# Another planned order for attention and two feed-forward stages, and x blocks at other addresses

## The chip, the cores and the metric

The kernel runs on one core of one Trainium2 chip. The metric is device time in microseconds (us) of one execution; of several executions the median counts.

## The reference

Three stages follow one another. First, block-causal attention over 4 batches, 8 heads, 576 positions and 64 values a head. Then a feed-forward with softmax-weighted linear units and a layer norm on 2304 tokens (512 to 1024 to 512), and a second feed-forward with Mish (512 to 2048 to 512).

```python
scores = scale * np.matmul(q, k.transpose(0, 1, 3, 2))     # masked by blocks of 64 positions
attn = softmax(scores); x = np.matmul(attn, v)             # to (2304, 512)
...
h = x @ w_in; solu = h * softmax(h)
ln = (solu - mean) / sqrt(var + 1e-06) * g_ln; x = ln @ w_out
...
h = x @ w2_in; g = h * tanh(softplus(h)); out = g @ w2_out
```

Inputs are float32, the weights float64.

## The kernel before

**Arithmetic.** Every large matmul is made of three in a shorter float format: an operand is split into a high part and the remainder (`h` and `l`), and high x high, low x high and high x low are summed in PSUM. The weights arrive as pairs of 32-bit words and are put together on the chip by a chain of some ten operations on DVE (VectorE), ACT (ScalarE) and POOL (GpSimd): L423 and L425 take the exponent and the mantissa apart, L467 and L477 to L482 put them together, L319, L325 and L328 split them.

**Stages.** Attention goes over 16 pairs of heads (`pair`, index p): loads of K, Q and V by SP, turns of K and Q on PE (TensorE) at L640, scores at L665, maxima on DVE, exponentials on ACT (L677), scaling on POOL (L733), turns of the result (L749) and the product with V (L770, L777). The first feed-forward takes 18 tiles of 128 tokens (`moe1_tile`: L833, L880) and 9 groups of two (`moe1_x2`: L896). Its result goes to DRAM. The second feed-forward (`moe2_group`, `moe2_pair`) goes in two halves over the hidden dimension; each half has five token groups (512, 512, 256, 512 and 512 tokens) and four pairs of hidden tiles. It computes the first product by a scheme of seven block products in place of eight (`prod`, L1055: six matmuls of 256 columns each), with ACT copies (L1063) and DVE adds (L1067) between them, then Mish, a split on ACT and DVE, and the output matmuls of 512 columns (L1112). Where a group has 256 tokens there are four products.

**The x blocks.** `moe2_x` reads x from DRAM (L1127), takes differences on DVE (L1132), and splits seven blocks into high parts (ACT, L319) and low parts (POOL, L328). They go to ten rotating buffers of each kind, `blk_h` and `blk_l`: 0 to 5 in the pool opened on the right after attention, 6 and 7 in the room of the first feed-forward's weights `wih` and `wil`, 8 and 9 in the pool opened on the left. Each buffer of the two pools is 528 values long, of which 512 are used, so that neighbours differ by 64 bytes modulo 512. The weights of the second feed-forward all start at 192 modulo 512. Blocks 0 to 5 start at 192, 256, 320, 384, 448 and 0 (both kinds), blocks 6 and 7 at 64 and 128, the high parts 8 and 9 at 192 and 256, and the low parts 8 and 9 at 320 and 384.

**The order.** Nothing in the program's order is written by hand. `add` collects operations (3 to 24 instructions of one engine for PE, mostly one for the others) with an engine, a cost in us, the keys read and written, a priority `prio`, and the PSUM banks they take and give back. `Plan.order` replays them in planned time: each engine takes, of the operations that are ready, the one with the lowest priority number. The result is a static order: on the chip each engine's instructions run in that order, and an instruction that waits holds all that stand behind it on its engine. An operation counts as ready when its inputs have ended and a latency of the producing engine has passed (`LAT`: PE, DVE, ACT, POOL, SP, host). The costs are formulas in the number n of values a partition (`c_dve`, `c_act`, `c_ts` and `c_tt` for POOL, `c_dma`). Operations of DVE with `lock`, most of those with operands in SBUF alone, and all of POOL hold one common lock, so that planned time never has one of DVE beside one of POOL.

**Priorities.** `PRIO` gives each tag a base and a step; the priority is base + step x index, the index being the pair of heads, the tile, the weight chunk (0 to 31) or the pair of tiles of the second feed-forward (0 to 39). Tags with `_b` belong to the pairs from 8 on. The tags of which the text speaks: `load_k`, `load_q`, `load_v` (SP), `wir`, `wor`, `w2ar`, `w2br` (reads of weights, SP), `wi`, `wo`, `w2a`, `w2b` (their conversion; `w2a` is for the first two sets of the second feed-forward), `f_x`, `f_t`, `f_s` (x: reads, differences, splits), `f_h` (products), `f_c` (copies), `f_d` (adds), `f_v`, `f_p`, `f_q` (Mish and the split of the hidden values), `f_o` (output matmuls).

The step that the adds take in `moe2_pair`:

```python
add(DVE, c_dve(256), lambda: nc.vector.tensor_tensor(
    out=part(x, i), in0=ps(s)[:, 0:256], in1=part(x, i), op=ALU.add),
    r=[key], w=[x.key(i)], rel=rel, prio=pri("f_d", cnt))
```

Of the kernel before, what the change touches and what calls it, by code (L numbers as in the profile page):

```python
# [26 lines left out]
PRIO = {  # L27
    "load_k": (3584270706, 49.53508582), "load_q": (3584552413, 2.997211538), "load_v": (3584552852, 30.17666404),
# [6 lines left out]
    "w2b": (3584800363, 0.1223531397), "m_x": (3584270481, -7.359126932), "m_h": (3584466166, -2.254093813),  # L35
    "m_v": (3584270377, 9.357429256), "m_w": (3584557870, 6.33404786), "m_u": (3584465474, 5.654352939),
    "m_s": (3584597059, 68.68855867), "m_l": (3584472153, 4.127067276), "m_t": (3584270485, -1.604672924),
    "m_e": (3584598271, 13.20145894), "m_2": (3584466906, 1.251409589), "m_o": (3584597866, 3.694405243),
    "store": (3584271882, 2.346070517), "load_k_b": (3584466375, -0.4078997786),
    "load_q_b": (3584466378, 0.8395418885), "load_v_b": (3584559519, -2.172838748), "tr_b": (3584270603, 85.63069486),  # L40
    "te_b": (3584466669, 21.88305874), "sc_b": (3584464169, 134.7168412), "mx_b": (3584598175, 8.054664166),
    "ex_b": (3584270568, 1.479017813), "su_b": (3584598230, 0.00851345384), "nm_b": (3584552091, 66.60840871),
    "pt_b": (3584270636, -0.9432254557), "pe_b": (3584270488, 0.2673815775), "pv_b": (3584464031, 70.47618497),
    "po_b": (3584269612, 69.4503458), "f_x": (3584558387, 3.529061523), "f_t": (3584466403, -0.8489929687),
    "f_s": (3584552262, 55.84067482), "f_h": (3584559956, 25.46036702), "f_c": (3584270484, -0.9543860343),
    "f_d": (3584269368, 3.538408075), "f_v": (3584464336, 40.97717236), "f_p": (3584465168, 9.220698474),
    "f_q": (3584466866, 0.03331880098), "f_o": (3584589259, 357.8175481), "f_a": (3584465747, 4.127067276),
    "f_e": (3584271879, 2.346070517),
}
# [17 lines left out]
class Plan:  # L67

    LAT = (0.21, 0.07, 0.07, 0.1, 2.4, 0.0)

# [196 lines left out]
def c_tt(n):  # L269
    return (110 + 2.3 * n) / 960.0  # L270


@with_exitstack
def kernel(
# [26 lines left out]
    NBLK = 10  # L301
    EDGE = 104
    NRIGHT = 6
# [91 lines left out]
    def weight(raws, ems, src, tag, idx, paths, after=(), pair=False):  # L395
# [21 lines left out]
        def dst():  # L417
# [4 lines left out]
            r=after, w=[rk], prio=pri(tag + "r", idx))  # L422
        add(DVE, (78 + wd / 2) / 960, lambda: nc.vector.tensor_scalar(ex(), hi(), 0x7FF00000, None, op0=ALU.bitwise_and),  # L423
            r=[rk], w=[ek], prio=pri(tag, idx), lock=True)
        add(DVE, (78 + wd / 2) / 960, lambda: nc.vector.tensor_scalar(  # L425
            ma(), hi(), 0xFFFFF, 0x100000, op0=ALU.bitwise_and, op1=ALU.bitwise_or), r=[rk], w=[mk], prio=pri(tag, idx), lock=True)
# [150 lines left out]
    def pair(p, xt):  # L577
        b, h2 = divmod(p, HP)

        def pri(tag, i):  # L580
            base, step = PRIO[tag if p < 8 else tag + "_b"]
            return base + step * i
# [85 lines left out]
        def sums(ts):  # L668
            a, n_ = ts
            c = [sm.key(x, t) for x in range(2) for t in range(a, a + n_)]  # L670
            add(DVE, 0.12, lambda: nc.vector.tensor_scalar(
                sm.t[:, :, a:a + n_], sm.t[:, :, a:a + n_], 1e-9, None, op0=ALU.add), w=c, prio=pri("su", p))
            add(DVE, 0.1, lambda: nc.vector.reciprocal(sm.t[:, :, a:a + n_], sm.t[:, :, a:a + n_]), w=c, prio=pri("su", p))  # L673
# [130 lines left out]
    def moe1_tile(i, xts, lth, ltl):  # L804
# [40 lines left out]
        def both(t):  # L845
# [6 lines left out]
            r=[hk, st.key(0)], w=[st.key(2), e.key()], prio=pri("m_w", i))  # L852
        add(DVE, 0.12, lambda: nc.vector.tensor_scalar(c(2), c(2), 1e-9, None, op0=ALU.add), w=[st.key(2)], prio=pri("m_u", i))
        add(DVE, 0.12, lambda: nc.vector.reciprocal(c(2), c(2)), w=[st.key(2)], prio=pri("m_u", i))
# [3 lines left out]
        add(DVE, 0.12, lambda: nc.vector.tensor_scalar(c(4), c(4), -1.0 / DFF, None, op0=ALU.mult),  # L858
            w=[st.key(4)], prio=pri("m_u", i))
# [3 lines left out]
        add(DVE, 0.12, lambda: nc.vector.tensor_scalar(c(6), c(6), 1.0 / DFF, 1e-6, op0=ALU.mult, op1=ALU.add),  # L863
            w=[st.key(6)], prio=pri("m_s", i))
# [86 lines left out]
    def open_right():  # L951
# [11 lines left out]
        for r in (blk_h, blk_l):  # L963
# [12 lines left out]
    def open_left():  # L976
# [4 lines left out]
        for j in range(3, NSLOT):  # L981
            slot(p, j)
        for r in (gh_r, gl_r, blk_h, blk_l, ob_r):
            r.make(p)
        for r in (blk_h, blk_l):
            r.tiles = [t[:, 0:512] for t in r.tiles]

# [47 lines left out]
    def moe2_pair(cnt, half, g, m, first, last, xs, oslots):  # L1035
# [12 lines left out]
        def prod(k, a, b, s, key, start):  # L1048
            xb, xl = xs[b]

            def go():
# [226 lines left out]
```

## Time and profile before

| what | value |
|---|---|
| median of 3 runs | 809.52 us (806.14, 811.68, 809.52) |
| profiled execution | 808.99 us |
| its span, first to last instruction | 807.2 us |
| mean granted clock of PE | 0.989 of 2.4 GHz |
| busy: PE, DVE, ACT, POOL | 781.4, 516.4, 442.8, 309.2 us |
| DMA | 69.38 MB |

The span is the time from the first to the last instruction of the profiled execution; some 1.8 us lie around it. A busy time is the union of an engine's instructions. A matmul's shown duration is longer than its share of the stream, because matmuls overlap: the pace is read from one start to the next. The granted clock is 1 at 2.4 GHz and 0.5 at 1.2 GHz.

### The profile page before, as it was taken

To read this page: it belongs to the slowest core of one execution; us is meant where nothing else is said; L and a number is where in the kernel's file an instruction comes from. 1 tells how busy PE (TensorE), PEld (TensorE's weight loads), DVE (VectorE), ACT (ScalarE), POOL (GpSimd) and SP (SyncE) were. 2 spreads that over 40 slices of the span, in tenths; PEclk is the share of its full clock that TensorE was granted. 3 is DMA by queue.
4 is the path that set the end of the run, shared out by engine and by line. 5 is a ranking of instruction groups with operands and counts; after the bars stand their busy time and mean duration, and the time that the engine had idled before them with its cause. 6 is when DMAs were issued, how large, how long until landed. Compare 5 with 4: busy or idle time off the path is not lost.

```text
span 807.2 us, 14839 instructions
## 1 busy us (share of the span) xinstructions
PE 781.4 (97%) x5700; PEld 692.1 (86%) x5700; DVE 516.4 (64%) x972; ACT 442.8 (55%) x988; POOL 309.2 (38%) x350
## 2 busy tenths in 40 slices
PE   7999998999999999999999899999999999999998
PEld 6877877779888988999998788999888989898886
DVE  6888988899644999333778774234896742532522
ACT  5888978678564654333746445345655634243431
POOL 2378778656433724312324425004153332200300
PEclk9999999999999999999999899999999999999999
DMA  7745471433012233000322433001424250310111
GB/s 154 169 127 138 113 184 43 116 96 119 14 44 66 83 114 105 27 27 28 105 81 90 130 119 105 1 27 53 143 79 157 66 165 19 131 37 18 40 53 53
DMA packets 93159, 69.38 MB, mean 86 GB/s; under 512 B 64160, under 2 KB 77984, under 8 KB 93088
## 3 DMA queue, kind: packets, MB, share of 16 engines
q1 hardware_dynamic: 91824, 68.12, 29.6%
q8 instruction: 45, 0.74, 0.4%
q10 hardware_dynamic: 1264, 0.31, 0.2%
q14 instruction: 26, 0.21, 0.1%
HBM read 54.25 MB, written 14.16 MB: 85 GB/s over the span
## 4 chain that ended last, share of the span: by engine, by line
PE 76%; DVE 14%; ACT 4%; issue 3%; DMA 1%; POOL 1%; SPq 0%; ACTq 0%; DVEq 0%; POOLq 0%
PE ps L1112 22%; PE ps L1055 22%; PE ps L833 10%; PE ps L896 10%; PE ps L749 3%; PE ps L665 3%; PE ps L770 3%; DVE nmx L719 2%; ACT pt L677 2%; PE ps L880 2%; DVE wem L425 1%; DVE wem L423 1%; PE ps L777 1%; DVE xf L1132 1%; DVE ptw L755 1%
## 5 line engine op out<-in xcount | busy, mean ns | idle before, releaser
L1067 DVE TENSOR_TENSOR xt<-ps,xt 128x256 f32<-128x256 f32 x104 | 43.9, 423 | 132.4 <-PE ps L1055 128.7
L733 POOL TENSOR_SCALAR pt<-pt,sm 128x192 f32<-128x192 f32 (+4 forms) x160 | 88.7, 575 | 59.7 <-DVE sm L673 22.6
L328 POOL TENSOR_TENSOR xbl<-xf,xbh 128x512 fp32r<-128x512 f32 x48 | 69.7, 1468 | 87.1 <-ACT xbh L319 68.2
L1055 PE MATMUL ps<-xbh,w2ih 128*128 128x256 f32 x312 | 92.9, 298 | 5.3 <-DVE xt L1067 2.9
L677 ACT ACTIVATE pt<-ps,nmx 128x448 f32<-128x448 f32 (+4 forms) x160 | 82.4, 535 | 25.5 <-DVE nmx L719 16.5
L482 POOL TENSOR_TENSOR wem<-wem 128x512 f32<-128x512 f32 x40 | 56.3, 1409 | 100.0 <-DVE wem L479 66.1
L1063 ACT ACTIVATE xt<-ps 128x256 f32<-128x256 f32 x104 | 39.3, 379 | 98.8 <-PE ps L1055 88.0
L1055 PE MATMUL ps<-xbl,w2ih 128*128 128x256 f32 x312 | 88.4, 283 | 0.0
L1055 PE MATMUL ps<-xbh,w2il 128*128 128x256 f32 x312 | 88.2, 283 | 0.0
L896 PE MATMUL ps<-lth,woh 128*128 128x256 f32 x288 | 81.2, 282 | 0.0
L896 PE MATMUL ps<-lth,wol 128*128 128x256 f32 x288 | 80.7, 280 | 0.0
L896 PE MATMUL ps<-ltl,woh 128*128 128x256 f32 x288 | 80.7, 280 | 0.0
L1055 PEld LDWEIGHTS ps<-xbh,w2ih 128*128 128x128 f32 x312 | 59.5, 191 | 9.6 <-ACT xt L1063 3.6
L1055 PEld LDWEIGHTS ps<-xbl,w2ih 128*128 128x128 f32 x312 | 59.8, 192 | 1.0
L1055 PEld LDWEIGHTS ps<-xbh,w2il 128*128 128x128 f32 x312 | 59.7, 191 | 0.0
L328 POOL TENSOR_TENSOR wil<-xf,wih 128x512 fp32r<-128x512 f32 x12 | 15.8, 1332 | 107.0 <-ACT wih L319 107.0
L896 PEld LDWEIGHTS ps<-lth,wol 128*128 128x128 f32 x288 | 55.0, 191 | 0.0
L896 PEld LDWEIGHTS ps<-lth,woh 128*128 128x128 f32 x288 | 54.1, 188 | 0.7 <-ACT pt L677 0.2
L896 PEld LDWEIGHTS ps<-ltl,woh 128*128 128x128 f32 x288 | 54.1, 188 | 0.3
L749 PE MATMUL ps<-ident,pt 128*128 128x128 f32 x400 | 50.2, 278 | 3.7 <-DVE kl L325 3.5
L749 PEld LDWEIGHTS ps<-ident,pt 128*128 128x128 f32 x400 | 45.6, 144 | 7.1 <-DVE kl L325 3.5
L833 PE MATMUL ps<-wih,xh 128*128 128x512 f32 x144 | 46.6, 405 | 0.2 <-ACT kh L319 0.2
(146 smaller groups left out, 2244.0 us busy)
## 6 DMA issues: line engine op xcount, KB each, us to landing
wraw<-in_moe_w_in_dram SPq DMA_DIRECT2D x24, 512.0 KB, 4.3
wraw<-in_moe_w_out_dram SPq DMA_DIRECT2D x24, 512.0 KB, 3.5
xf<-x_d SPq DMA_DIRECT2D x36, 256.0 KB, 2.9
qraw<-in_q_dram SPq DMA_DIRECT2D x30, 160.0 KB, 3.3
x_d<-xo SPq DMA_DIRECT2D x18, 256.0 KB, 2.3
acc_d<-ob SPq DMA_DIRECT2D x18, 256.0 KB, 2.0
ob<-acc_d SPq DMA_DIRECT2D x18, 256.0 KB, 3.6
out_dram<-ob SPq DMA_DIRECT2D x18, 256.0 KB, 2.0
```

The source lines that it names most:

```text
L328: nc.gpsimd.tensor_tensor(out=dst, in0=src, in1=hi.bitcast(F32), op=ALU.subtract)
L482: add(POOL, c_tt(wd), lambda: nc.gpsimd.tensor_tensor(out=mf(), in0=mf(), in1=ex().bitcast(F32), op=ALU.mult), r=[ek], w=[mk], **pt)
L665: nc.tensor.matmul(out=dst, lhsT=a.t[hs, t * P:(t + 1) * P], rhs=m.t[hs, o + c0:o + c1], start=(i == 0), stop=(i == 2))
L677: add(ACT, c_act(EXT[t], acc=True), lambda: nc.scalar.activation(out=pp.t[:, x * EXT[t]:(x + 1) * EXT[t]] if t < 4 else pp.t[:, x * EXT[t] ...
L733: nc.gpsimd.tensor_scalar(pp, pp, sm.t[:, x, t:t + 1], 1.0, op0=ALU.mult, op1=ALU.mult)
L749: nc.tensor.transpose(ps2(s)[:, a, o:o + P], pts[t].t[:, c * P:(c + 1) * P], ident)
L833: nc.tensor.matmul(out=ps2(hp)[:, hf, :], lhsT=x.t[:, kk, :], rhs=w[:, kk, hf * 512:(hf + 1) * 512], start=bool(first), stop=bool(last))
L896: nc.tensor.matmul(out=ps(s)[:, (c % 2) * 256:(c % 2) * 256 + 256], lhsT=w[:, kk, cs], rhs=x.t[:, kk, :], start=(kk == 0 and i == 0), stop ...
L1055: nc.tensor.matmul(out=ps(s)[:, 0:256], lhsT=sl_i[j, w][:, c, a, :], rhs=x.t[:, mv], start=(start and c == 0 and i == 0), stop=(c == 1 and ...
L1063: add(ACT, c_act(256), lambda: nc.scalar.activation(out=part(x, i), in_=ps(s)[:, 0:256], func=AF.Copy), r=[key] + need, w=[x.key(i)], prio ...
L1067: add(DVE, c_dve(256), lambda: nc.vector.tensor_tensor(out=part(x, i), in0=ps(s)[:, 0:256], in1=part(x, i), op=ALU.add), r=[key], w=[x.key ...
L1112: nc.tensor.matmul(out=ps(oslots[t]), lhsT=x.t[:, tsl], rhs=sl_o[j, wk][:, jj, :], start=(first and jj == 0 and i == 0), stop=(last and jj ...
```

## The change

No operation is added to the kernel or taken out of it. Three things change.

1. `PRIO` is replaced as a whole, and the pairs of heads 0 and 1 get tags of their own (`_a`). The replays with random durations of which the change's name speaks are not part of the kernel; only the numbers are.
2. The planner's costs and latencies change: `LAT` of DVE, ACT and POOL goes up, the fixed parts of the costs go down, and two of PE's costs go up a little.
3. The blocks lie without gaps at 128 modulo 512, 64 bytes below the weights: a filler of 448 bytes stands ahead of them in both pools, the two in `wih` and `wil` start at 2928 in place of 2912, and the left pool takes its output buffers (`ob`) first.

```diff
-    "load_k": (3584270706, 49.53508582), "load_q": (3584552413, 2.997211538), "load_v": (3584552852, 30.17666404),
...
-    "wi": (3584658969, -18964.76747), "wor": (3584558466, -9.112298009), "wo": (3584558608, 3.429909476),
-    "w2ar": (3584466206, 11.49880019), "w2a": (3584597868, 2.383904164), "w2br": (3584558683, -3.587062681),
-    "w2b": (3584800363, 0.1223531397), "m_x": (3584270481, -7.359126932), "m_h": (3584466166, -2.254093813),
...
-    "po_b": (3584269612, 69.4503458), "f_x": (3584558387, 3.529061523), "f_t": (3584466403, -0.8489929687),
-    "f_s": (3584552262, 55.84067482), "f_h": (3584559956, 25.46036702), "f_c": (3584270484, -0.9543860343),
-    "f_d": (3584269368, 3.538408075), "f_v": (3584464336, 40.97717236), "f_p": (3584465168, 9.220698474),
-    "f_q": (3584466866, 0.03331880098), "f_o": (3584589259, 357.8175481), "f_a": (3584465747, 4.127067276),
...
+    "pv_a": (3584448949, -5.34337149), "po_a": (3584457941, 19.79257215), "load_k": (3584461400, 68.55638698),
+    "load_q": (3584459310, 9.330330335), "load_v": (3584463276, 69.84320077), "tr": (3584449754, 312.4690727),
...
+    "po": (3584467645, -2.140577887), "wir": (3584461316, 7.970762078), "wi": (3584463579, 566.8655893),
+    "wor": (3584459543, 0.380854314), "wo": (3584466292, 2.453296928), "w2ar": (3584459540, 0.380854314),
+    "w2a": (3584452869, 164.9630977), "w2br": (3584467096, 24.15585328), "w2b": (3584466024, 4.873065304),
...
+    "f_x": (3584459130, 0.1450497809), "f_t": (3584452950, -3.281526728), "f_s": (3584459476, 13.54428432),
+    "f_h": (3584461186, 5.289585339), "f_c": (3584453247, 2.844727618), "f_d": (3584466289, -7.102560702),
+    "f_v": (3584458042, 24.81877839), "f_p": (3584459573, 13.54428432), "f_q": (3584451499, 5.753656382),
+    "f_o": (3584464285, 6.601970345), "f_a": (3584458951, 12.88440484), "f_e": (3584451434, 12.0016119),
...
-    LAT = (0.21, 0.07, 0.07, 0.1, 2.4, 0.0)
+    LAT = (0.21, 0.21, 0.18, 0.16, 2.4, 0.0)
...
 def c_dve(n):
-    return (78 + 1.03 * n) / 960.0
+    return (64 + 1.02 * n) / 960.0
 def c_act(n, sbuf=False, acc=False, ptr=False):
-    return 0.076 + n / 1160.0 + 0.04 * sbuf + 0.18 * acc + 0.09 * ptr
+    return 0.05 + n / 1170.0 + 0.04 * sbuf + 0.18 * acc + 0.09 * ptr
 def c_ts(n):
-    return (100 + 1.08 * n) / 960.0
+    return (85 + 1.08 * n) / 960.0
 def c_tt(n):
-    return (110 + 2.3 * n) / 960.0
+    return (80 + 2.28 * n) / 960.0
...
-            base, step = PRIO[tag if p < 8 else tag + "_b"]
+            base, step = PRIO[tag + ("_a" if p < 2 else "" if p < 8 else "_b")]
...
-                    add(PE, 12 * 0.115, lambda s=s, c=2 * c2 + cc, k0=k0: mm(s, c, k0, k0 + 4),
+                    add(PE, 12 * 0.1175, lambda s=s, c=2 * c2 + cc, k0=k0: mm(s, c, k0, k0 + 4),
...
-            add(PE, 0.7, go, r=[("w2i", j, c, x) for c in range(2) for x in "hl"] + [xb.key(), xl.key()]
+            add(PE, 0.706, go, r=[("w2i", j, c, x) for c in range(2) for x in "hl"] + [xb.key(), xl.key()]
...
-    EDGE = 104
+    EDGE = 88
-    blk_h = Rot(None, "xbh", NBLK, (P, 512 + 16), F32R)
-    blk_l = Rot(None, "xbl", NBLK, (P, 512 + 16), F32R)
+    blk_h = Rot(None, "xbh", NBLK, (P, 512), F32R)
+    blk_l = Rot(None, "xbl", NBLK, (P, 512), F32R)
...
         xf_r.make(p)
+        p.tile([P, 112], F32, name="edge_f")
         blk_h.make(p, NRIGHT)
-        p.tile([P, 32], F32, name="edge_f")
         blk_l.make(p, NRIGHT)
         p.tile([P, EDGE], F32, name="edge_g")
...
-            r.tiles += [flat[:, 2912 + 528 * i:3424 + 528 * i] for i in range(2)]
+            r.tiles += [flat[:, 2928 + 512 * i:3440 + 512 * i] for i in range(2)]
...
-        for r in (gh_r, gl_r, blk_h, blk_l, ob_r):
+        for r in (gh_r, gl_r, ob_r):
             r.make(p)
+        p.tile([P, 112], F32, name="edge_h")
         for r in (blk_h, blk_l):
-            r.tiles = [t[:, 0:512] for t in r.tiles]
+            r.make(p)
```

## Rows read from the trace of the kernel before

**Rows 1.** The page's first part: span, and busy us with share and count.

```profile
span 807.2 us, 14839 instructions
...
PE 781.4 (97%) x5700; PEld 692.1 (86%) x5700; DVE 516.4 (64%) x972; ACT 442.8 (55%) x988; POOL 309.2 (38%) x350
```

**Rows 2.** Engines by stage: stretch, length, busy us, PE's clock, DMA share, GB/s.

```profile
0.00:30.00 30.00, 24.03 (x187) 21.31 (x189) 20.29 (x57) 19.43 (x52) 10.46 (x25) 0.89 0.81 168
30.00:200.00 170.00, 161.49 (x1565) 134.31 (x1562) 154.42 (x322) 136.53 (x357) 116.23 (x159) 0.99 0.46 117
395.00:470.00 75.00, 71.27 (x468) 65.01 (x467) 57.95 (x93) 42.83 (x83) 25.42 (x18) 0.95 0.34 104
470.00:600.00 130.00, 129.17 (x805) 116.21 (x805) 71.67 (x125) 67.17 (x145) 35.33 (x25) 1.00 0.24 72
600.00:615.00 15.00, 13.29 (x80) 11.48 (x79) 9.89 (x11) 7.15 (x15) 8.86 (x7) 1.00 0.39 122
```

**Rows 3.** Waits of PE: who waits for whom, us in total, times, longest.

```profile
PE ps L640 <- ACT pt L677: 4.0, 5, 1.6
PE ps L1055 <- DVE xt L1067: 3.7, 4, 1.5
...
PE ps L1055 <- ACT xt L1063: 2.5, 4, 1.9
...
PE ps L640 <- DMA kraw<-in_k_dram: 0.6, 1, 0.6
```

**Rows 4.** Timeline, 441 to 449 us: start, length, instruction, idle before and releaser.

```profile
441.10 0.69 DVE L325 TENSOR_TENSOR gl<-xt,gh 128x512 fp32r<-128x512 f32 x1
...
441.70 6.68 POOL L328 TENSOR_TENSOR xbl<-xf,xbh 128x512 fp32r<-128x512 f32 x4 [3.99 <-ACT xbh L319]
...
445.74 1.52 DVE L423 TENSOR_SCALAR wem<-wraw 128x512 int32<-128x512 int32 x1
...
447.19 1.48 DVE L425 TENSOR_SCALAR wem<-wraw 128x512 int32<-128x512 int32 x1
...
447.93 0.36 ACT L1063 ACTIVATE xt<-ps 128x256 f32<-128x256 f32 x1
...
448.34 0.38 PE L1055 MATMUL ps<-xbh,w2ih 128*128 128x256 f32 x1 [1.89 <-ACT xt L1063]
```

**Rows 5.** Engines in 452 to 456 us, columns as in rows 2.

```profile
452.00:456.00 4.00, 4.00 (x17) 3.74 (x17) 0.85 (x2) 0.94 (x2) 0.00 (x0) 0.50 0.46 131
```

**Rows 6.** Timeline, 606 to 607 us: an add and the matmuls behind it.

```profile
606.09 0.41 DVE L1067 TENSOR_TENSOR xt<-ps,xt 128x256 f32<-128x256 f32 x1
...
606.55 0.39 PE L1055 MATMUL ps<-xbh,w2ih 128*128 128x256 f32 x1 [1.46 <-DVE xt L1067]
606.77 0.28 PE L1055 MATMUL ps<-xbl,w2ih 128*128 128x256 f32 x1
```

**Rows 7.** Timeline of PE: first matmul of three products and of the one behind.

```profile
444.19 0.28 PE L1055 MATMUL ps<-wih,w2ih 128*128 128x256 f32 x1
...
444.90 0.28 PE L1055 MATMUL ps<-xbh,w2ih 128*128 128x256 f32 x1
...
493.57 0.28 PE L1055 MATMUL ps<-xbh,w2ih 128*128 128x256 f32 x1
...
494.30 0.28 PE L1055 MATMUL ps<-xbh,w2ih 128*128 128x256 f32 x1
...
723.37 0.28 PE L1055 MATMUL ps<-wih,w2ih 128*128 128x256 f32 x1
...
724.05 0.34 PE L1055 MATMUL ps<-xbh,w2ih 128*128 128x256 f32 x1
```

**Rows 8.** SP's waits (us in total, times, longest), and DMA issues of K.

```profile
SPq L421 <- DVE wem L479: 54.0, 12, 9.0
...
kraw<-in_k_dram SPq DMA_DIRECT2D x16, 160.0 KB, 3.0
```

**Rows 9.** Groups of DVE's instructions: the adds, busy us, mean ns, idle before.

```profile
L1067 DVE TENSOR_TENSOR xt<-ps,xt 128x256 f32<-128x256 f32 x104 | 43.9, 423 | 132.4 <-PE ps L1055 128.7 <-ACT xt L1063 3.4
```

More of the change, by code (lines that the diff above doesn't have):

```diff
@@ L27 @@
 PRIO = {
-    "load_k": (3584270706, 49.53508582), "load_q": (3584552413, 2.997211538), "load_v": (3584552852, 30.17666404),
[6 rows of a table removed]
-    "w2b": (3584800363, 0.1223531397), "m_x": (3584270481, -7.359126932), "m_h": (3584466166, -2.254093813),
-    "m_v": (3584270377, 9.357429256), "m_w": (3584557870, 6.33404786), "m_u": (3584465474, 5.654352939),
-    "m_s": (3584597059, 68.68855867), "m_l": (3584472153, 4.127067276), "m_t": (3584270485, -1.604672924),
-    "m_e": (3584598271, 13.20145894), "m_2": (3584466906, 1.251409589), "m_o": (3584597866, 3.694405243),
@@ L39 @@
[L39 to L43, printed above, removed]
@@ L44 @@
-    "po_b": (3584269612, 69.4503458), "f_x": (3584558387, 3.529061523), "f_t": (3584466403, -0.8489929687),
-    "f_s": (3584552262, 55.84067482), "f_h": (3584559956, 25.46036702), "f_c": (3584270484, -0.9543860343),
-    "f_d": (3584269368, 3.538408075), "f_v": (3584464336, 40.97717236), "f_p": (3584465168, 9.220698474),
-    "f_q": (3584466866, 0.03331880098), "f_o": (3584589259, 357.8175481), "f_a": (3584465747, 4.127067276),
-    "f_e": (3584271879, 2.346070517),
+    "load_k_a": (3584451969, 0.7748023), "load_q_a": (3584457898, 43.7181896), "load_v_a": (3584465318, 17.58187057),
@@ new lines @@
+    "tr_a": (3584461254, -6.373456343), "te_a": (3584453026, 3.482077194), "sc_a": (3584459313, 142.6656332),
+    "mx_a": (3584459260, 1.664159439), "ex_a": (3584465692, 5.09675985), "su_a": (3584459661, 0.9156984346),
+    "nm_a": (3584459454, 4.304473418), "pt_a": (3584466017, 8.518471271), "pe_a": (3584459305, 10.15229961),
+    "pv_a": (3584448949, -5.34337149), "po_a": (3584457941, 19.79257215), "load_k": (3584461400, 68.55638698),
+    "load_q": (3584459310, 9.330330335), "load_v": (3584463276, 69.84320077), "tr": (3584449754, 312.4690727),
[6 rows of a table added]
@@ new lines @@
+    "m_x": (3584467550, 0.06992002774), "m_h": (3584459582, 13.31637089), "m_v": (3584450548, 4.470325821),
+    "m_w": (3584467613, 0.5214435792), "m_u": (3584466044, 12.583851), "m_s": (3584451747, 2.903461847),
+    "m_l": (3584461241, 1.81090621), "m_t": (3584459155, 2.066182601), "m_e": (3584452656, -8.438701903),
+    "m_2": (3584459786, 85.82973234), "m_o": (3584468142, -5.011302989), "store": (3584451509, 0.5640087274),
+    "load_k_b": (3584452078, 2.389215478), "load_q_b": (3584458911, 14.2540699),
@@ new lines @@
+    "load_v_b": (3584451199, 90.08067166), "tr_b": (3584452512, -2.677940006), "te_b": (3584451458, 2.113223735),
+    "sc_b": (3584459293, -0.3310616743), "mx_b": (3584452888, 1.233323849), "ex_b": (3584451458, 2.41870934),
+    "su_b": (3584431384, 2252.961107), "nm_b": (3584469012, 2.431108073), "pt_b": (3584451992, 559.1652553),
+    "pe_b": (3584469207, 13.10436393), "pv_b": (3584451882, 13.11669194), "po_b": (3584451319, -9.747046996),
+    "f_x": (3584459130, 0.1450497809), "f_t": (3584452950, -3.281526728), "f_s": (3584459476, 13.54428432),
@@ L422, in weight @@
             r=after, w=[rk], prio=pri(tag + "r", idx))
-        add(DVE, (78 + wd / 2) / 960, lambda: nc.vector.tensor_scalar(ex(), hi(), 0x7FF00000, None, op0=ALU.bitwise_and),
+        add(DVE, (66 + wd / 2) / 960, lambda: nc.vector.tensor_scalar(ex(), hi(), 0x7FF00000, None, op0=ALU.bitwise_and),
             r=[rk], w=[ek], prio=pri(tag, idx), lock=True)
-        add(DVE, (78 + wd / 2) / 960, lambda: nc.vector.tensor_scalar(
+        add(DVE, (66 + wd / 2) / 960, lambda: nc.vector.tensor_scalar(
             ma(), hi(), 0xFFFFF, 0x100000, op0=ALU.bitwise_and, op1=ALU.bitwise_or), r=[rk], w=[mk], prio=pri(tag, idx), lock=True)
@@ L670, in sums @@
             c = [sm.key(x, t) for x in range(2) for t in range(a, a + n_)]
-            add(DVE, 0.12, lambda: nc.vector.tensor_scalar(
+            add(DVE, 0.075, lambda: nc.vector.tensor_scalar(
                 sm.t[:, :, a:a + n_], sm.t[:, :, a:a + n_], 1e-9, None, op0=ALU.add), w=c, prio=pri("su", p))
@@ L852, in moe1_tile @@
             r=[hk, st.key(0)], w=[st.key(2), e.key()], prio=pri("m_w", i))
-        add(DVE, 0.12, lambda: nc.vector.tensor_scalar(c(2), c(2), 1e-9, None, op0=ALU.add), w=[st.key(2)], prio=pri("m_u", i))
-        add(DVE, 0.12, lambda: nc.vector.reciprocal(c(2), c(2)), w=[st.key(2)], prio=pri("m_u", i))
+        add(DVE, 0.075, lambda: nc.vector.tensor_scalar(c(2), c(2), 1e-9, None, op0=ALU.add), w=[st.key(2)], prio=pri("m_u", i))
+        add(DVE, 0.075, lambda: nc.vector.reciprocal(c(2), c(2)), w=[st.key(2)], prio=pri("m_u", i))
         add(DVE, c_dve(1024) + 0.05, lambda: nc.vector.scalar_tensor_tensor(
@@ L857, in moe1_tile @@
             accum_out=c(4)), r=[hk, st.key(2)], w=[st.key(4), e.key()], rel=[hp], prio=pri("m_u", i))
-        add(DVE, 0.12, lambda: nc.vector.tensor_scalar(c(4), c(4), -1.0 / DFF, None, op0=ALU.mult),
+        add(DVE, 0.075, lambda: nc.vector.tensor_scalar(c(4), c(4), -1.0 / DFF, None, op0=ALU.mult),
             w=[st.key(4)], prio=pri("m_u", i))
@@ L862, in moe1_tile @@
             w=[st.key(6), jk.key()], prio=pri("m_s", i))
-        add(DVE, 0.12, lambda: nc.vector.tensor_scalar(c(6), c(6), 1.0 / DFF, 1e-6, op0=ALU.mult, op1=ALU.add),
+        add(DVE, 0.075, lambda: nc.vector.tensor_scalar(c(6), c(6), 1.0 / DFF, 1e-6, op0=ALU.mult, op1=ALU.add),
             w=[st.key(6)], prio=pri("m_s", i))
@@ L958, in open_right @@
         xf_r.make(p)
+        p.tile([P, 112], F32, name="edge_f")
         blk_h.make(p, NRIGHT)
-        p.tile([P, 32], F32, name="edge_f")
         blk_l.make(p, NRIGHT)
         p.tile([P, EDGE], F32, name="edge_g")
-        for r in (blk_h, blk_l):
-            r.tiles = [t[:, 0:512] for t in r.tiles]
     def open_mid():
@@ L982, in open_left @@
             slot(p, j)
-        for r in (gh_r, gl_r, blk_h, blk_l, ob_r):
+        for r in (gh_r, gl_r, ob_r):
             r.make(p)
+        p.tile([P, 112], F32, name="edge_h")
         for r in (blk_h, blk_l):
-            r.tiles = [t[:, 0:512] for t in r.tiles]
+            r.make(p)
     def slot_gate(j):
```

7 rows, old and new, of the table PRIO are left out of this document.

## The prediction

> **What bounds the kernel now.** I read the page's busy line first, then a table of the engines by stage, the list of TensorE's waits, and last the timeline around the two stretches where TensorE stands longest. TensorE (PE) is busy 781.4 of 807.2 us, 97%; DVE is next with 64% [rows 1]. So the end is set by PE, and a new order can only win what PE loses: the 25.8 us in which it is idle, the stretches at the lower of its two clocks (1.2 in place of 2.4 GHz), and whatever its matmuls take over their fastest pace.
>
> Where it loses them is in the table by stage [rows 2]. In the first 30 us PE is idle 6.0 us and the granted clock is 0.89, which costs 0.11 x 30 = 3.3 us more. From 30 to 200 us (attention) 8.5 us are idle and 0.01 x 170 = 1.7 us go to the clock. From 395 to 470 us (the start of the second feed-forward) 3.7 us are idle and 0.05 x 75 = 3.75 us go to the clock. From 600 to 615 us (its second half starts) 1.7 us are idle. Between 470 and 600 us there are only 0.8 us in 130: once the weights are converted the order holds.
>
> The list of waits [rows 3] says what ends these gaps. In attention it is above all ACT's exponentials (4.0 us); in the second feed-forward DVE's adds at L1067 (3.7 us) and ACT's copies at L1063 (2.5 us). DMA is 0.6 us.
>
> The timeline shows why the later gaps are so long [rows 4]. From 441.70 us POOL runs four splits of x in one piece of 6.68 us. Meanwhile DVE's weight conversions at L423 and L425 take 1.52 and 1.48 us, although a 512-column operation of DVE on SBUF took 0.69 us just before (441.10). The planner marks all of these with one lock, so its plan never has them side by side; on the chip they came side by side, and DVE gave way. ACT's copy behind them starts at 447.93, and the product that needs it at 448.34 after an idle time of 1.89 us. A few microseconds later the granted clock is 0.50 for a whole 4 us window in which PE is busy all the time [rows 5]. So one collision cost its idle time twice over. At 601 to 606 us the same pattern costs 1.46 us without the clock [rows 6].
>
> **The change part by part.** No instruction is added or removed: the same matmuls, copies, splits and DMAs in another order on each engine, and x blocks at other addresses.
>
> *The block addresses.* The second feed-forward has 256 products of six 256-column matmuls (8 pairs of f tiles, 7 products for each of four token groups and 4 for the short one, so 8 x 32). The trace leaves out buffer numbers. Counted through the program's order, the product at 493.57 us reads block 4, which lies 256 bytes above its weights modulo 512, and takes 494.30 - 493.57 = 0.73 us (six starts 0.12 apart); the product at 723.37 us reads block 7, the one block of the ten that already lies 64 bytes below its weights, and takes 0.68 us [rows 7]. Block 7 does not always do this: its product at 444.19 us takes 0.71 us, and of 152 undisturbed products, counted so from 395 us to the end, most lie between 0.70 and 0.72 whatever their block. The bounds are therefore a loss of 256 x 0.01 = 2.6 us (block 7's usual 0.71 against the 0.70 of the best others) and a gain of 256 x 0.05 = 12.8 us (every product goes from the slowest of these rows to the fastest). I take a gain of 1.5 us, 0.006 us a product, by the row at 444.19, which is the usual one: a pace like that at 723.37 is rare even for block 7.
>
> The Trainium skill speaks against any gain here: its page "TensorE: Matmul & The Clock Gate", section "Part 2: What happens when you issue a matmul", gives TensorE two independent read ports of SBUF, one for the moving operand and one for the weights, so that their relative address should not matter. By that the term would be 0 and the sum 802.0 us. The two products above differ by 0.05 us, which by that rule needs another cause.
>
> *The planner's constants.* An add at L1067 starts at 606.09 us, PE's weight load that waited for it at 606.55, and the next matmul comes 0.22 us behind the first, not 0.12 as in a stream: 0.46 + 0.10 = 0.56 us until the stream runs again [rows 6]. The old constants plan this hop with 0.356 + 0.07 = 0.43 us, the new ones with 0.339 + 0.21 = 0.55 us. ACT's copy: 448.34 - 447.93 = 0.41, and 0.51 with the same restart [rows 4]; old 0.37, new 0.45. The next DVE operation starts before the last one's end is shown (447.19 against 445.74 + 1.52 = 447.26 [rows 4]), so an occupancy shorter than the shown duration is right too. The new plan therefore leaves PE's queue room where the old one cut each hop 0.13 us short. A product placed too early on PE holds every matmul behind it, since the queue is in order.
>
> *The order.* What it can return in the two starts of the second feed-forward is 3.7 + 3.75 + 1.7 = 9.15 us [rows 2]. Nothing at all, or a loss of as much again, is the other end. I take 6.0 us: the clock's share (3.75 us), which goes if the stall ahead of it does, and of the 5.4 us of idle time somewhat under a half. In attention 8.5 + 1.7 = 10.2 us could come back; there the gaps are many and under 1 us each, at DVE 91% busy (154.4 of 170 us [rows 2]), so the order has little room: I take 1.0 us, between -5 and +5. The first 30 us I leave as they are: the loads and the first exponentials set them. What is late next, when a stall goes, is the matmul stream itself.
>
> *What is moved, queue by queue.* On DVE the adds (f_d) were first of all; now they rank behind the splits of the hidden values (f_q), the differences (f_t), and, for the first sixteen pairs, behind every weight conversion. I cost that at nothing: there are 104 adds at 0.42 us [rows 9], DVE is busy 71.7 of 130 us between 470 and 600 us [rows 2], and the 24 output matmuls of another pair, some 24 x 0.24 = 5.8 us by twice the 256-column pace of rows 7, lie ready on PE to cover a late add. If that cover is gone, each add waits for one more operation, 0.4 to 1.5 us. On POOL the splits of x move ahead of the first feed-forward's work, and only the late weight conversions stay behind: cover as before. On SP the K and V loads of pairs 2 to 7 now rank behind every weight read. A weight read waits up to 9.0 us for its buffer, and a K load takes 3.0 us to land [rows 8]; in order, a K load behind a waiting weight read is late. Bounds: 0, and 6 pairs x 3.0 = 18 us. I take 0, because PE's whole wait for K is 0.6 us now [rows 3].
>
> *The sum.* The profiled execution took 808.99 us (span 807.2 and 1.8 around it), 0.5 below the median of 809.52. 808.99 - 6.0 - 1.0 - 1.5 = 800.5 us, 1.1% below the median.
>
> **The rivals.**
> *The stalls move.* A static order meets a collision wherever DVE and POOL drift apart, and POOL's work keeps its length (35.3 us of it between 470 and 600 us alone [rows 2]). For it: the old plan had the same lock and collided all the same. Against it: rows 4 and 6 are two places, not many. Only the block term stays: 807.5 us.
> *Slower: adds behind conversions.* The place is the conversion of the six weight sets m = 2 to 7, where DVE now does conversions before adds. Price: each set holds an add once behind a stretched operation, as at 446 us (1.89 us [rows 4]), so 6 x 1.9 = 11.4 us of idle time in place of 5.4, and two more drops of the clock at the 3.75 us of the one seen [rows 2]: 808.99 + 6.0 + 7.5 - 1.5 = 821.0 us. It decides from the point where idle time in these stretches exceeds 5.4 + 1.5 us. For it: the ranking; against it: PE's ready output matmuls.
> *Much faster.* Both collisions go whole (9.15), half of attention's loss (5.1), the first 30 us keep the full clock (3.3) and the blocks give 1.5: 808.99 - 19 = 790 us. For it: the constants now fit the rows; against it: DVE's load in attention.
> *The address does nothing.* The forecast without the block term: 802.0 us. For it: most products of all blocks lie within 0.02 us of each other; against it: rows 7.
>
> **How the numbers follow.** The forecast gets 0.42, with a range of its own of 795 to 806 us; the moved stalls 0.25; slower 0.10; much faster 0.18; the idle address 0.05. One per cent, 8.1 us, is about what a measurement of this kernel can tell from no change; so faster means under 801.4 us and slower over 817.6. Faster: somewhat over half of the forecast (0.24), the 0.18, and 0.05 from the edges of the others: 0.47. Slower: 0.10. The rest, 0.43, is the same. The range runs from 788 (much faster, with 2 us more from the blocks) to 813 us (a collision more than now, without the second drop of the clock); it leaves out the slower rival and the far end of the fast one, under 2 in 10.
>
> **What would show it right or wrong.** Right: a clock row of 1.00 in every window after 200 us; idle time of PE under 3 us from 395 to 615 us; no conversion of DVE over 1 us beside a piece of POOL in these starts; six-matmul products at 0.71 us or less throughout. Wrong: PE idle before L1055 on the adds at L1067 with over 5 us (the slower rival); waits of L640 for the K load over 3 us (SP's order); a granted clock of 0.50 anywhere after 30 us (the stalls moved); the same spread of product times as now (the address).

## The result and the profile after

The changed kernel takes 787.71 us (median of 4, 787.42 to 789.4) beside 808.82 us for the kernel before (median of 4): ratio 0.9743, 95% interval 0.9706 to 0.978. That is 21.1 us less, 2.6%. The forecast was 800.5 us with a range from 788 to 813: the direction was right, the size less than half of what came, and the time lies just outside the range.

The busy line of the page after, which answers to [rows 1]:

```profile
span 785.7 us, 14886 instructions
...
PE 765.3 (97%) x5700; PEld 681.5 (87%) x5700; DVE 510.5 (65%) x972; ACT 445.4 (57%) x988; POOL 313.2 (40%) x350
```

PE does the same 5700 matmuls and is busy 16.1 us less. (The page counts 47 instructions more than before; all are semaphore instructions.) This is the line to stop at: an order was expected to remove idle time, and idle time fell only from 25.8 to 20.4 us. Three quarters of the gain lie in time that the page counts as busy.

The stages after, with the columns of [rows 2]. The second feed-forward's first product starts at 387.5 us (394.4 before), so the windows from 395 us on are moved by 7 us:

```profile
0.00:30.00 30.00, 22.87 (x191) 19.84 (x193) 21.39 (x62) 19.84 (x53) 12.03 (x26) 0.94 0.79 177
30.00:200.00 170.00, 163.99 (x1585) 137.21 (x1582) 155.87 (x317) 136.09 (x353) 120.24 (x161) 1.00 0.48 120
...
388.00:463.00 75.00, 72.10 (x496) 66.06 (x496) 59.01 (x100) 44.77 (x88) 27.66 (x20) 1.00 0.35 109
463.00:593.00 130.00, 129.54 (x826) 117.18 (x826) 71.43 (x127) 68.68 (x146) 39.41 (x28) 1.00 0.23 72
593.00:608.00 15.00, 14.88 (x89) 13.00 (x88) 11.03 (x23) 11.03 (x22) 4.85 (x4) 1.00 0.70 239
```

The clock is full in every window after 30 us. From 463 to 593 us, where before and after both have under 1 us of idle time, PE now does 826 matmuls in 130 us; it was 805. That stage has no idle time to give, and still does 2.1% more work, a matmul of 512 columns counted as two of 256.

PE's waits after, in us, times, longest [rows 3]:

```profile
PE ps L753 <- DVE kl L329: 3.6, 8, 0.6
PE ps L1058 <- DVE xt L1070: 2.3, 4, 1.7
PE ps L644 <- ACT pt L681: 2.2, 3, 1.2
...
PE ps L1058 <- ACT xt L1066: 1.0, 1, 1.0
...
PE ps L644 <- DMA kraw<-in_k_dram: 0.7, 1, 0.7
```

**Where the busy time went.** A matmul's real cost is the time to the next start. Summed that way, the matmuls of the second feed-forward (L1055 and L1112, now L1058 and L1115) fell from 400.7 to 386.5 us, 14.2 us; all the others from 405.1 to 397.7 us, 7.4 us. The timeline of the kernel before shows the largest part of the 14.2 us. An add on DVE ends at 519.70 + 0.42 = 520.12 us, and the product that waits for it starts at 520.18. (By the program a product reads nothing that an add writes. It waits for the PSUM bank that the add reads.) PEld is TensorE's weight load:

```profile
519.70 0.42 DVE L1067 TENSOR_TENSOR xt<-ps,xt 128x256 f32<-128x256 f32 x1 [2.54 <-PE ps L1055]
...
520.05 0.28 PE L1055 MATMUL ps<-xbh,w2il 128*128 128x256 f32 x1
...
520.17 0.19 PEld L1055 LDWEIGHTS ps<-xbh,w2ih 128*128 128x128 f32 x1
520.18 0.39 PE L1055 MATMUL ps<-xbh,w2ih 128*128 128x256 f32 x1
...
520.40 0.28 PE L1055 MATMUL ps<-xbl,w2ih 128*128 128x256 f32 x1
```

No idle time stands on the row at 520.18, because it begins before the shown end of the matmul at 520.05. But its own duration is 0.39 us, not 0.28, and the next start comes 0.22 us later, not 0.12. The wait is hidden inside a longer "busy" matmul. What came late is the weight load. In the stream it starts with the matmul ahead, about 0.11 us before its own matmul; here it had to wait and starts 0.01 us before. I call this a gap and count a product's matmul as one when the next start comes 0.17 to 0.24 us after it, outside the stretches of half clock. The kernel before has 52 of them, 5.7 us over the pace of 0.113 us; the changed one has 11, 1.2 us. In 42 of the 52 the weight load waited for an add and starts 0.05 to 0.06 us after its end; in 9 it waited for a copy.

From start to start over the paces of 0.113 us (256 columns) and 0.226 us (512 columns), the 14.2 us are, up to rounding: 4.5 from these gaps, 1.5 from smaller delays of the same matmuls (next start after 0.13 to 0.17 us; 80 before, 31 after), 4.2 from the half clock around 449 us, 1.7 from longer stalls, and 2.2 from the pace of the undisturbed matmuls.

The changed kernel puts work between. The add at 510.33 us ends at 510.75; three output matmuls run meanwhile, the weight load comes 0.22 us ahead, and the product that waits starts at 511.45, with 0.12 us to the next:

```profile
510.33 0.42 DVE L1070 TENSOR_TENSOR xt<-ps,xt 128x256 f32<-128x256 f32 x1 [2.38 <-PE ps L1058]
...
510.77 0.39 PE L1115 MATMUL ps<-w2oh,gh 128*128 128x512 f32 x1
...
511.23 0.19 PEld L1058 LDWEIGHTS ps<-xbh,w2ih 128*128 128x128 f32 x1
...
511.45 0.28 PE L1058 MATMUL ps<-xbh,w2ih 128*128 128x256 f32 x1
...
511.57 0.28 PE L1058 MATMUL ps<-xbl,w2ih 128*128 128x256 f32 x1
```

### The profile page after: what moved, and what is told of

Its sections match the earlier page's. It is cut to its first block, busy times and chain, and to the rows that moved or that the text cites. A ratio compares the mean times of both kernels' runs of the same rounds, so it can differ in the third digit from the quotient of the medians.

```text
span 785.7 us, 14886 instructions
## 1 busy us (share of the span) xinstructions
PE 765.3 (97%) x5700; PEld 681.5 (87%) x5700; DVE 510.5 (65%) x972; ACT 445.4 (57%) x988; POOL 313.2 (40%) x350
## 4 chain that ended last, share of the span: by engine, by line
PE 78%; DVE 13%; ACT 4%; issue 2%; DMA 1%; POOL 0%; SPq 0%; DVEq 0%; ACTq 0%; POOLq 0%
PE ps L1115 21%; PE ps L1058 20%; PE ps L900 13%; PE ps L837 12%; PE ps L669 3%; PE ps L753 3%; PE ps L774 3%; DVE nmx L723 2%; PE ps L884 2%; ACT pt L681 2%; DVE ptw L759 1%; DVE wem L471 1%; DVE wem L483 1%; PE ps L781 1%; DVE wem L429 1%
## 5 line engine op out<-in xcount | busy, mean ns | idle before, releaser
L737 POOL TENSOR_SCALAR pt<-pt,sm 128x192 f32<-128x192 f32 (+4 forms) x160 | 91.2, 590 | 46.2 <-DVE sm L677 23.6
L681 ACT ACTIVATE pt<-ps,nmx 128x192 f32<-128x192 f32 (+4 forms) x160 | 82.3, 536 | 17.3 <-DVE nmx L723 12.2
L1058 PE MATMUL ps<-xbh,w2ih 128*128 128x256 f32 x312 | 89.0, 285 | 1.6 <-ACT xt L1066 1.0
L486 POOL TENSOR_TENSOR wem<-wem 128x512 f32<-128x512 f32 x40 | 54.0, 1352 | 87.3 <-DVE wem L483 47.7
L1058 PE MATMUL ps<-xbl,w2ih 128*128 128x256 f32 x312 | 87.4, 280 | 0.0
L1058 PE MATMUL ps<-xbh,w2il 128*128 128x256 f32 x312 | 87.4, 280 | 0.0
L1058 PEld LDWEIGHTS ps<-xbh,w2ih 128*128 128x128 f32 x312 | 58.6, 188 | 5.5 <-DVE xt L1070 1.8
L1058 PEld LDWEIGHTS ps<-xbl,w2ih 128*128 128x128 f32 x312 | 58.7, 188 | 1.9
L1058 PEld LDWEIGHTS ps<-xbh,w2il 128*128 128x128 f32 x312 | 59.5, 191 | 0.0
L753 PEld LDWEIGHTS ps<-ident,pt 128*128 128x128 f32 x400 | 44.0, 141 | 8.5 <-DVE kl L329 3.4
```

The lines of the kernel that those rows point to most:

```text
L486: add(POOL, c_tt(wd), lambda: nc.gpsimd.tensor_tensor(out=mf(), in0=mf(), in1=ex().bitcast(F32), op=ALU.mult), r=[ek], w=[mk], **pt)
L681: add(ACT, c_act(EXT[t], acc=True), lambda: nc.scalar.activation(out=pp.t[:, x * EXT[t]:(x + 1) * EXT[t]] if t < 4 else pp.t[:, x * EXT[t] ...
L737: nc.gpsimd.tensor_scalar(pp, pp, sm.t[:, x, t:t + 1], 1.0, op0=ALU.mult, op1=ALU.mult)
L753: nc.tensor.transpose(ps2(s)[:, a, o:o + P], pts[t].t[:, c * P:(c + 1) * P], ident)
L1058: nc.tensor.matmul(out=ps(s)[:, 0:256], lhsT=sl_i[j, w][:, c, a, :], rhs=x.t[:, mv], start=(start and c == 0 and i == 0), stop=(c == 1 and ...
```

## The experiments

Twelve kernels ran. Each ratio is to the kernel before, run beside it on the same chip: its median there was 809.16 us for e1 to e4, 807.51 for e5 to e8 and 808.58 for e9 to e12. The changed kernel was run beside 808.82 us, so medians of different groups differ by a few tenths for that alone. "Second" and "others" are the sums from start to start of one profiled execution, as above; two executions of one kernel can differ there by some 2 us, as the clock drops at other places (e1 keeps the order of the kernel before and shows 407.4 for 405.1 in "others").

| run | median us | ratio to before, interval | gaps | second us | others us |
|---|---|---|---|---|---|
| before | 808.82 | | 52 | 400.7 | 405.1 |
| changed | 787.71 | 0.9743 (0.9706 to 0.978) | 11 | 386.5 | 397.7 |
| e1: before, new addresses | 807.6 | 0.9984 (0.9967 to 1.0002) | 62 | 400.0 | 407.4 |
| e2: changed, old addresses | 790.81 | 0.9766 (0.9744 to 0.9787) | 10 | 389.0 | 398.2 |
| e3: before, new costs and latencies | 808.41 | 0.9995 (0.9978 to 1.0012) | 6 | 386.5 | 420.3 |
| e4: changed, old costs and latencies | 823.56 | 1.0174 (1.0148 to 1.0199) | 52 | 391.0 | 427.3 |
| e5: changed, old latencies | 819.18 | 1.014 (1.0113 to 1.0167) | 64 | 398.1 | 418.2 |
| e6: before, new latencies | 811.04 | 1.004 (1.0023 to 1.0056) | 13 | 393.9 | 416.6 |
| e7: changed, no lock | 844.76 | 1.0468 (1.0451 to 1.0485) | 26 | 413.6 | 428.3 |
| e8: changed, old priorities in the second part | 784.94 | 0.9725 (0.9711 to 0.974) | 10 | 384.1 | 398.0 |
| e9: before, new latency of the adds | 805.04 | 0.9945 (0.9924 to 0.9966) | 12 | 396.5 | 405.4 |
| e10: before, new latencies in the second part | 798.13 | 0.986 (0.9827 to 0.9892) | 7 | 392.9 | 403.5 |
| e11: changed, old latency of the adds | 794.14 | 0.9817 (0.979 to 0.9843) | 63 | 392.9 | 398.2 |
| e12: e10 with the new addresses | 795.87 | 0.9838 (0.9812 to 0.9865) | 14 | 389.0 | 404.6 |

### Order or address

Theory A: the order. Theory B: the gaps come from the addresses. Addresses don't enter the planner, so e1 and e2 exchange them alone: the filler, the block length, the two blocks in `wih` and `wil`, and the place of `ob`.

```diff
-            r.tiles += [flat[:, 2912 + 528 * i:3424 + 528 * i] for i in range(2)]
+            r.tiles += [flat[:, 2928 + 512 * i:3440 + 512 * i] for i in range(2)]
```

> The old order with the new block addresses; no instruction changes its place. Theory A (the order brings nearly all of the gain, the address only evens the pace of the six-matmul products from about 118.9 to 117.6 ns a matmul): 1.5 us less than before, 806 to 808 us, ratio 0.998, and the first matmul of some 50 products still starts the next one about 0.22 us later, as before. Theory B (those 0.1 us gaps at the start of products come from the address, the x block and the weights getting in each other's way): 52 such gaps fall to about 11 and the 80 smaller ones to about 31, 6 us more off, 799 to 802 us, ratio 0.99.

> The new order with the old block addresses. Theory A: 1.5 us more than the changed kernel, 788 to 791 us, and still about 11 gaps of 0.1 us at the start of products. Theory B: 794 to 798 us, with 40 to 50 such gaps.

e1 took 807.6 us with 62 gaps, e2 790.81 us with 10. B falls: the number of gaps follows the order, not the address. What the address does is in the pace. Summed over the matmuls that are within 15 ns of 0.113 us (0.226 for the output matmuls), the time over that pace fell in e1 from 9.1 to 6.0 us, and it is 9.7 us in e2 against 6.9 in the changed kernel (and 9.8 in e10 against 6.7 in e12, below): some 3 us each time. No run moves the blocks without `ob` and the fillers, so that the offset to the weights is what counts is argued, not shown. In e1 little of it reached the end (1.3 us by the ratio, an interval that includes none); its profiled execution had one drop of the clock more than before, at 607 us.

### Costs and latencies, or priorities

e3 gives the kernel before the new constants; e4 gives the changed kernel the old ones.

```diff
-    LAT = (0.21, 0.07, 0.07, 0.1, 2.4, 0.0)
+    LAT = (0.21, 0.21, 0.18, 0.16, 2.4, 0.0)
...
 def c_dve(n):
-    return (78 + 1.03 * n) / 960.0
+    return (64 + 1.02 * n) / 960.0
```

> Old priorities and addresses, with the new costs and latencies of the planner. If the planner's latencies by themselves take the work apart that stood too close (theory C), the 0.1 us gaps fall from 52 to under 20 and the time goes to 797 to 802 us whatever the priorities. If the priorities were needed with them (theory D), the old numbers give an order that is no better than before, 804 to 818 us.

> New priorities and addresses, with the old costs and latencies of the planner. Theory C: most of the gain is lost, 798 to 806 us, and the 0.1 us gaps come back to 40 or more. Theory D: the priorities carry the gain, 788 to 794 us, with few gaps.

As a forecast of the whole, both theories miss: e3 is as fast as before, as D said, but with 6 gaps, as C said; e4 is slower than either, which neither said, with 52 gaps. The two sums tell it apart. In the second feed-forward C holds whatever the priorities: 386.5 us with the old ones, the very value of the changed kernel. In the first part the old priorities take 15.2 us more under the new constants than under their own, and the new ones 29.6 us more under the old constants than under theirs: there numbers and constants only work together.

In e4 much of that loss is one place, the output matmuls of the first feed-forward, which wait for their weights. Its waits of PE, and its window:

```profile
PE ps L900 <- ACT woh L503: 11.3, 3, 5.0
...
PE ps L900 <- DVE wol L505: 3.7, 3, 2.2
```

```profile
157.70:178.20 20.50, 8.21 (x28) 6.46 (x29) 15.03 (x24) 6.66 (x11) 11.97 (x14) 0.50 0.34 102
```

PE is busy 8.2 of 20.5 us and the granted clock is 0.50 throughout.

e5 and e6 exchange `LAT` alone, the first line of the diff above.

> The changed kernel with only the old latencies of DVE, ACT and POOL; the new cost formulas stay. If the latencies make the 0.1 us gaps at the start of products (theory C1), 40 or more of them come back (11 in the changed kernel, 52 and 62 in the two orders made with the old model) and the second feed-forward's matmuls take 390 us or more, not 386.5. If the lower costs did it (theory C2), the gaps stay under 20. The time of the whole also holds what the first part's order does: 790 to 806 us.

> The kernel before with only the new latencies. Theory C1: under 20 gaps of 0.1 us, and the second feed-forward's matmuls at 386 to 389 us in place of 400.7, as when costs and latencies were both new (386.5). Theory C2: over 40 gaps and over 395 us. The first part loses its order as it did there, so that the whole stays at 802 to 815 us.

The gaps follow the latencies (64 and 13): C1 holds. Two sizes missed. e5 is 819 us, not 806 at most, because the first part lost 20.5 us; and e6's second part is 393.9 us, not 389 at most, since stalls and a drop of the clock at 462 us remain in it.

### The surgical ones

e9 and e11 change one number, the latency of the adds at L1067 (0.21 in e9, 0.07 in e11). PE's order stays that of the kernel that it was made from until the second feed-forward has begun; behind that, 396 of PE's 5700 places hold a matmul of other tiles in e9, and 345 in e11.

```diff
-                r=[key], w=[x.key(i)], rel=rel, prio=pri("f_d", cnt))
+                r=[key], w=[x.key(i)], rel=rel, prio=pri("f_d", cnt), lat=0.21)
```

> The kernel before with one number changed: the planner's latency of the adds (L1067) alone is 0.21 in place of 0.07 us; all else is planned as before. Of the 52 gaps of 0.1 us in the kernel before, 42 stand behind such an add. If that latency is their cause, the gaps fall under 20 and the time by 3 to 6 us, to 802 to 806 us. If other waits take their place, they stay over 35 and the time within 2 us of before.

> The changed kernel with the latency of the adds alone back at 0.07 us. If that latency is the cause of the gaps, over 35 of them come back (11 in the changed kernel) and the time rises by 3 to 6 us, to 790 to 794 us. If not, 786 to 789 us.

e9: 12 gaps and 0.55% less, 4.5 us of 808.6. e11: 63 gaps and 794.14 us, 6.4 us more than the changed kernel. One number, both ways, as forecast, except that e11 lies just over its range.

The numbers of the plan say how it works, here for the add at 519.70 us. Between the product whose sum the add reads and the product that waits for the add lies one other product, 0.70 us in the plan. With the old numbers the second is ready 0.21 + 0.356 + 0.07 = 0.64 us after the first, in time to be planned right behind the one between. With 0.21 for the add's latency (e9) it is 0.78 us, too late, so the planner takes other work first. On the chip it took 0.75 us, from the end of the first in the stream (the next product starts at 519.42) to the weight load at 520.17.

The group of the first matmuls of each term shows it without a count. Its columns are busy us and mean ns of one; the kernel before has 92.9 and 298. e9, then the changed kernel, then e11:

```profile
L1055 PE MATMUL ps<-xbh,w2ih 128*128 128x256 f32 x312 | 90.4, 290 | 5.6 <-ACT xt L1063 3.1 <-DVE xt L1067 2.3
```

```profile
L1058 PE MATMUL ps<-xbh,w2ih 128*128 128x256 f32 x312 | 89.0, 285 | 1.6 <-ACT xt L1066 1.0 <-DVE xt L1070 0.4
```

```profile
L1058 PE MATMUL ps<-xbh,w2ih 128*128 128x256 f32 x312 | 92.1, 295 | 1.8 <-ACT xt L1066 1.4 <-DVE xt L1070 0.2
```

Between the changed kernel and e11 the idle time is the same to 0.2 us, and the mean is 10 ns longer: the wait sits in the duration.

e10 gives the new latencies to all operations of the second feed-forward, and e12 the addresses as well. The weight conversions among them run beside the first part, so the order there changes too:

```diff
     early = len(plan.ops)
+    plan.LAT = (0.21, 0.21, 0.18, 0.16, 2.4, 0.0)
```

> The kernel before with the new latencies for the operations of the second feed-forward alone (its weight conversions with them); the first part's order, the old costs, priorities and addresses stay. If the latencies carry the gain of the second feed-forward, its matmuls take 386 to 391 us in place of 400.7, with under 20 gaps, and the whole 796 to 800 us. If the lower costs or the priorities are needed too, over 394 us and over 802 us.

> The same as the kernel before with the new latencies in the second feed-forward alone, and the new block addresses besides. If the parts add up, 2.5 to 3 us less than without the addresses: 793 to 797 us, and what is then left to the changed kernel, 6 to 8 us, is the order of the first part. If the parts overlap, within 1 us of the run without the addresses.

e10: 798.13 us; e12: 795.87 us, 2.3 us less. The whole lands where expected, and the parts add up but for some tenths. The second part's sum in e10, 392.9 us, is 2 us over what was expected: its profile still has a drop of the clock at 447 us.

### The priorities of the second part, and the lock

e8 puts the old values of all tags `f_`, of `w2b`, `w2br` and `store` into the changed kernel; e7 takes the common lock out of the planner.

```diff
-        o.lock = lock or eng == POOL
+        o.lock = False
```

> The changed kernel with the old priorities of the second feed-forward (all tags f_, the late weight reads and conversions, the stores), under the new costs, latencies and addresses. If the second feed-forward gained by the planner's latencies and not by its priorities (theory C), its matmuls stay at 384 to 390 us with under 20 gaps, and the whole at 785 to 791 us. If the new priorities were needed there (theory D), 793 us or more.

> The changed kernel with the planner's common lock of DVE and POOL taken out, so that planned time may have them side by side. If a collision of the two is what lengthens DVE's conversions and holds PE (as the rows at 441 to 448 us of the kernel before were read), the operations at the conversions' lines get longer on average and PE loses 5 us or more: 793 to 810 us. If the lock decides little, 786 to 791 us.

e8 took 784.94 us, with 10 gaps: the new priorities of the second part bring nothing, and the old ones under the new latencies are no worse. Its median is 2.8 us below the changed kernel's, but the intervals of the ratios overlap and the two were not run side by side, so it is a version at least as good, not one shown to be faster.

e7 took 844.76 us, far over its expected range: the plan without the lock is some 57 us slower. The expected sign is there, but small: the 176 operations at L427, L429, L471 and L483 take 711 ns on average in place of 684, nearly all of it at L427 (525 to 627). The differences of x at L1135 grow more. The changed kernel, then e7:

```profile
L1135 DVE TENSOR_TENSOR xf<-xf,xf 128x512 f32<-128x512 f32 x32 | 27.5, 860 | 2.5 <-POOL xbl L332 2.4
```

```profile
L1135 DVE TENSOR_TENSOR xf<-xf,xf 128x512 f32<-128x512 f32 x32 | 37.2, 1161 | 1.2 <-POOL xbl L332 1.0
```

The 64 operations at L1015 go from 372 to 451 ns. And e7's plan is another order altogether, so how much of the 57 us is collisions and how much the order isn't told apart by it.

## Why the prediction was right or wrong

**What bounds the kernel** was right: PE's time, and DMA and the other engines' busy time don't matter. What was wrong is the account of PE's losses. The step "a new order can only win what PE loses" named three items, and then valued two of them by idle time and clock. The third, what matmuls take over their fastest pace, was valued only for the addresses.

**The step that failed** is the planner's constants. It worked out the right hop from rows 6 (0.46 us to the wait's end, 0.10 more for the restart), found the old constants 0.13 us short, and then gave this no term in the sum. It also left the evidence aside: it counted 152 "undisturbed" products of 256, and of the 252 outside the half clock 49 took 0.79 to 0.82 us (10 of 256 after the change). The rows that it looked at were those with idle time; with "the matmul stream itself" taken as next in line, the 0.10 us was counted nowhere. In the two profiles the term is 6.0 us, the gaps and the smaller delays together. e9 and e11 measure the adds' part at 4.5 and 6.4 us, and e10 all of the second part's latencies at 11.3 us of 808.6 (ratio 0.986; 10.5 by the medians). That also holds idle time, which the prediction counted under the order, so it is not to be added to the next term.

**The order in the second part** (taken: 6.0 us). Idle time and clock gave what was said, and a little more: idle time from 5.4 to 2.9 + 0.1 us in the shifted windows and the clock's 3.75 us to none, 6.2 us. That the size fits so well is luck in part: in other executions the mean granted clock was 0.987 to 0.996 before and 0.993 to 0.998 after, so what the clock takes is not the same each time. The cause isn't the new ranking either, since e3 and e8 reach 386.5 and 384.1 us in the second part with the old priorities under the new constants. And the collisions are still there:

```profile
439.84 4.74 POOL L332 TENSOR_TENSOR xbl<-xf,xbh 128x512 fp32r<-128x512 f32 x3 [0.21 <-ACT xbh L323]
...
440.17 1.53 DVE L471 SCALAR_TENSOR_TENSOR wem<-wraw,wem 128x512 f32<-128x512 uint32 x1
...
441.62 1.79 DVE L483 SCALAR_TENSOR_TENSOR wem<-wraw,wem 128x512 int32<-128x512 int32 x1
```

PE has output matmuls and another product to do meanwhile and shows no idle time there. Of such conversions over 1 us beside POOL there are 14 from 395 to 615 us before and 12 from 388 to 608 us after. The order took away the wait behind the collision, not the collision. Of the signs forecast for it, the full clock came; no conversion over 1 us did not; idle time under 3 us was just missed (3.5 us from 395 to 615 us); and 0.71 us or less holds for 214 of the 256 products, where it was 112 of 252.

**The first part** (taken: 1.0 us for attention, none for the first 30 us) is the second term that failed, and its miss is as large: it gave 7.4 us in the sums. Between e12 and the changed kernel the sums give 6.9 us there and 2.5 in the second part; the ratios (0.9838 and 0.9743) give 7.7 for both. The reason for the small term, that attention's gaps are "many and under 1 us each", does not fit rows 3, where the 4.0 us behind the exponentials are five waits of up to 1.6 us; after the change they are three, 2.2 us. By the tables of stages, attention won 2.5 us of idle time and 1.7 of the clock; in the first 30 us the clock gave 1.5 us (0.06 x 30 where it was 0.11 x 30) and idle time took 1.2. Between 200 us and the second feed-forward idle time fell from 1.2 us to 0.1. The rest, some 1.7 us, no run takes apart. That it comes from the new priorities and constants together, and from neither alone, is shown by e3, e4 and e8; which tags do it stays open.

**The addresses** (taken: 1.5 us) can't be told from what was taken by the time alone: e1 measures 1.3 us in the old order, e12 against e10 2.3 us by the medians and 1.8 by the ratios, and the changed kernel against e2 3.1 and 1.9 us, and none of these is outside the noise of its intervals. The pace says some 3 us. The two independent read ports of the Trainium skill ("TensorE: Matmul & The Clock Gate", section "Part 2: What happens when you issue a matmul") would have made it nothing. The pace of the same order with other addresses, 9.7 against 6.9 us over the fastest, says that something that was moved counts; these runs do not show that it is the offset between the two operands.

**The rivals.** "Adds behind conversions" did not come: PE's wait for adds fell from 3.7 to 2.3 us although they now rank behind conversions, covered by output matmuls, as argued. K loads behind weight reads cost nothing (0.7 us for 0.6); the prediction has their place too low, since the late reads `w2br` still rank behind them. "Much faster" at 790 us was nearest in time, in part by luck. Attention gave 4.2 us of the 5.1 in its list, but the starts gave 6.2 of 9.15 and the first 30 us 0.3 of 3.3; the 6.0 us of gaps and smaller delays that made up for it are not in the list.

**The parts.** In the prediction's own terms, the 21.5 us between the two profiled executions are 6.0 for the constants (taken as nothing), 5.9 for stalls and clock in the second part (taken: 6.0), 2.2 for the pace (taken: 1.5, for the addresses) and 7.4 for the first part (taken: 1.0). By the ratios, from e9 to e10, e12 and the changed kernel, they are 0.55% for the adds' latency, 0.85% for the other latencies of the second part, 0.22% for the addresses and 0.95% for all else, mostly the first part's order. These four add up to 2.57% by the way they are formed, and each is uncertain by 0.2% or more.

## What to carry to other kernels

Before pricing an order, add up the time from one start to the next for each group of the engine that bounds, and compare it with the fastest pace: a wait that ends just as the queue runs dry is shown as a longer busy instruction, not as idle time. A static order made by a planner is only as good as the latencies it was made with; where a hop measured in the trace differs from the planner's constant, multiply the difference by the number of hops before anything else, as an upper bound (here 0.13 us x 104 adds = 13.5 us; e9 and e11 show 4.5 and 6.4). And priorities fitted to one set of constants need not survive another: e3 and e4 exchanged only the constants, and lost 15 and 30 us in the first part against the kernels that they come from.

## What was not expected of the hardware

A wait that ends just in time for a matmul is too late for its weight load, and costs 0.10 us: at 520 us the weight load starts 0.05 us after the add's shown end, its matmul 0.01 us later, and the matmul behind that 0.22 us later in place of 0.12. The collisions of DVE and POOL are as long after the change as before (1.53 and 1.79 us at 440 to 443 us, 1.48 to 1.78 us at 444 to 449 us before) and cost PE nothing where it has other work.

The pace of the output matmuls changed with the blocks' addresses, though they read none of the blocks: their time over 0.226 us fell from 2.0 to 1.1 us in e1, and is 2.3 us in e2 against 1.1 in the changed kernel. No run here shows why.
